# Two of the eight loads of a's rows per piece issued by GpSimd instead of SyncE

## The chip, the cores and the metric

The kernel runs on one core of a Trainium2 chip. The metric is the device time of one execution in microseconds (us), as the median of several executions. The engines of the core are TensorE (PE, its weight loads shown apart as PEld), VectorE (DVE), ScalarE (ACT), GpSimd (POOL) and SyncE (SP). DMA transfers are issued by SP or by POOL, each in the order of its own instruction stream, and run on the core's 16 DMA engines.

## What is computed

The reference, cut to what matters, for 8 batches, 8 heads, 576 positions, a head width of 64 and 32 memory slots:

```
a = exp(phi - max over positions);  a = a / (sum over positions + 1e-9)
k_m = einsum('bhsm,bhsd->bhmd', a, k)
v_m = einsum('bhsm,bhsd->bhmd', a, v)
attn = softmax over the 32 slots of (q @ k_m^T) / sqrt(64)
x = attn @ v_m, heads side by side: 8 x 576 x 512
score = x @ w_gate; of each batch the 128 rows with the highest score:
    x[row] += sigmoid(score) * (relu(x[row] @ w1) @ w2)
```

The change concerns `v_m`, the sum over the positions of a times v.

## The kernel before

Everything runs on one core, and the order of each engine's instructions is fixed when the program is built: generators (`batch`, `split_v`, `sums`, `attention_beside`, `load_weights`, `forward`) are stepped in turn by a loop at the end of the function, each with its own rate, and what they emit goes into the engines' streams in that order.

Per batch, `softmax` computes a on DVE and ACT. `keys` turns a round with PE (line 303), splits it into a coarse and a fine part (`aS` and `alo`), and stores both parts twice in the DRAM buffer `aparts` with eight DMAs from POOL (line 314). It also computes k_m with PE (line 322). `split_v` does the same for v: a load into `vb` on SP (line 271), the split on DVE, and stores to `vparts` from POOL (line 290).

`values` then computes v_m for a set of four batches at a time, so there are two stages of sums. A stage walks over the 576 positions in 24 pieces of T = 24 positions. Of a piece, `load` (lines 340 to 352) brings v's rows into the buffer `v_rows` with two DMAs of 384 KB from POOL (line 345), and a's rows into `a_rows` with eight DMAs of 48 KB from SP (line 350): four blocks `j`, two groups `g` each. There are two buffers of each kind (NB = 2). The piece is 96 small matmuls on PE (line 371), 24 for each of the four accumulators `acc`. `load` of piece c is written into the program after the first four matmuls of piece c-1, but it fills the buffer that piece c-2 has read, so SP and POOL wait for the last matmul of piece c-2 before they issue it. The pieces are numbered through here: 0 to 23 are the first stage, 24 to 47 the second.

Beside the loads of a's rows, SP issues all loads of inputs: `ph` (line 101), `kb` (105), `qb` (109), `vb` (271) and the weights. Beside the loads of v's rows, POOL issues the stores to `vparts` and `aparts`, the stores of the result (533) and the gathers and scatters of the chosen rows (594, 636). On each of the two queues there are eight semaphores for DMAs, used in turn: a DMA waits until the one issued eight places before it on its queue has landed.

In the first stage the sums alternate on PE with the keys of the batches 4 to 7; in the second with the attention of the batches 0 to 3 and the dense layers (lines 622, 629). After the second stage the attention of the batches 4 to 7 follows.

Of the kernel before, what the change touches and what calls it, by code (L numbers as in the profile page):

```python
# [44 lines left out]
def kernel(  # L45
# [14 lines left out]
    nc = tc.nc  # L60
# [273 lines left out]
    def values(st):  # L334

        accs = [accp.tile([P, 512], F32, name=f"acc{i}") for i in range(SET)]
        b0 = st * SET

        def load(ch):
            ss = slice(ch * T, (ch + 1) * T)
            vr, ar = v_rows[ch % NB].bitcast(F32), a_rows[ch % NB].bitcast(F32)
            for g in range(NG):
                nc.gpsimd.dma_start(  # L345
                    out=vr[g::2, :, g],
                    in_=vparts[g, b0:b0 + SET].rearrange("b t w j s d -> (b t w j) s d")[:, ss])
            for j in range(NPR):
                for g in range(NG):
                    nc.sync.dma_start(  # L350
                        out=ar[2 * j + g::8, j].rearrange("p s m -> p (s m)"),
                        in_=aparts[g, j, b0:b0 + SET].rearrange("b t w s m -> (b t w) (s m)")
                            [:, ch * T * M:(ch + 1) * T * M])


        n = S // T
        while len(keyed) < b0 + SET or min(split[b0:b0 + SET]) < NG * VC:
            yield
        for _ in range(4):
            yield  # L360
        for ch in range(NB - 1):
            load(ch)
            yield
        warm(warmth[st])
        yield
        for ch in range(n):
            vr, ar = v_rows[ch % NB], a_rows[ch % NB]
            for s in range(T):
                for bb in range(SET):
                    p = slice(bb * 32, bb * 32 + 32)  # L370
                    nc.tensor.matmul(out=accs[bb][:, :P].rearrange("p (j m) -> p j m", m=M),  # L371
                                     lhsT=vr[p, s].rearrange("p g d -> p (g d)"), rhs=ar[p, :, s],
                                     start=(ch == 0 and s == 0), stop=(ch == n - 1 and s == T - 1))
                if s == 0 and ch + NB - 1 < n:
                    load(ch + NB - 1)
                if s % 4 == 4 - 1:
                    yield
        for bb in range(SET):
            v_m[b0 + bb] = const.tile([P, P], F32, name=f"v_m{b0 + bb}")
            nc.scalar.activation(v_m[b0 + bb], accs[bb][:, :P], AF.Copy)  # L380
# [3 lines left out]
    def warm(n):  # L384

        if n:
            spare = bank([P, 512])
            for i in range(n):
                nc.tensor.matmul(out=spare, lhsT=ident16, rhs=wide[:, :512], start=True, stop=True)
# [406 lines left out]
```

## Time and profile before

| | us |
|---|---|
| median of 3 runs | 911.61 |
| the runs | 911.61, 912.07, 907.06 |
| the profiled execution | 907.15 |
| its span, first to last instruction | 905.3 |
| DVE busy in the span | 548.2 (61%) |
| PE busy in the span | 547.1 (60%) |
| POOL busy in the span | 258.7 (29%) |
| ACT busy in the span | 222.6 (25%) |
| mean rate of the DMAs | 183 GB/s |

The profiled execution is at the lower edge of the runs; 1.85 us of it lie outside the span. No engine is busy all the time. Up to 251 us DVE is busy nearly throughout with the softmaxes of the first batches; the two stages of sums run from 251 to 450 and from 475 to 721 us; the rest is attention and dense layers on PE and DVE. The profile puts a wait down to what ended it, and shows the chain of work that ended last, followed back from the end.

### The profile page before, as it was taken

The page shows a single profiled execution, that of the slowest core. Times are in us where ns is not written, and L with a number is a line of the kernel's source. Part 1 is how long each engine was busy: PE and PEld are TensorE (multiplying, and loading weights), DVE is VectorE, ACT ScalarE, POOL GpSimd, SP SyncE. Part 2 cuts the span into 40 slices and gives each one's busy share as a digit, 9 for nine tenths or more (in the row PEclk, how much of TensorE's full clock was granted, in tenths as well). Part 3 has the DMA queues.
Part 4 walks back from the last instruction along what each step waited for, and adds up shares of the span by engine and source line. Part 5 has one row for each costly group of instructions (what it writes and reads, how often), then busy time and mean ns, then how long its engine had stood idle before and what let it go on. Part 6 is the DMA issues. An engine that isn't in the chain of part 4 may idle for free.

```text
span 905.3 us, 16762 instructions
## 1 busy us (share of the span) xinstructions
PE 547.1 (60%) x6917; PEld 449.3 (50%) x6918; DVE 548.2 (61%) x803; ACT 222.6 (25%) x369; POOL 258.7 (29%) x373
## 2 busy tenths in 40 slices
PE   0010020202066568774859999987999798598595
PEld 0010020202065568774728787865885675476373
DVE  8997999999965386655914336206225347748800
ACT  2423242525213124222310120300210223134210
POOL 7245353425335224224142213223223011101100
PEclk9999999999999555557585555868569799589888
DMA  3569899896998677857777755546255433111200
GB/s 103 169 246 321 267 310 293 268 306 228 292 266 259 173 226 233 225 172 210 239 214 224 233 171 167 159 125 209 69 165 175 123 94 99 64 38 64 76 21 18
DMA packets 61409, 165.55 MB, mean 183 GB/s; under 512 B 12816, under 2 KB 21008, under 8 KB 61328
## 3 DMA queue, kind: packets, MB, share of 16 engines
q0 software_dynamic: 30080, 108.02, 37.2%
q1 hardware_dynamic: 31248, 56.39, 21.3%
q8 instruction: 57, 0.93, 0.4%
q14 instruction: 24, 0.20, 0.1%
HBM read 96.21 MB, written 68.16 MB: 182 GB/s over the span
## 4 chain that ended last, share of the span: by engine, by line
PE 45%; DVE 27%; DMA 15%; SPq 5%; issue 4%; POOL 1%; ACT 1%; DVEq 0%; POOLq 0%; ACTq 0%
PE acc L371 19%; PE bank L622 8%; DMA a_rows<-aparts 7%; PE bank L629 5%; SPq L350 5%; PE bank L522 4%; DMA aparts<-aS 3%; PE bank L505 3%; DVE mx L183 2%; DMA vparts<-vlo 2%; DVE vlo L287 2%; PE bank L585 2%; DVE ph L252 2%; DMA aparts<-alo 1%; PE bank L303 1%
## 5 line engine op out<-in xcount | busy, mean ns | idle before, releaser
L371 PE MATMUL acc<-a_rows,v_rows 32*128 32x128 f32 x4608 | 234.5, 374 | 114.1 <-DMA a_rows<-aparts 87.8
L371 PEld LDWEIGHTS acc<-a_rows,v_rows 32*128 32x128 f32 x4608 | 220.0, 285 | 142.6 <-issue 125.3
L345 POOL DMA_DIRECT2D v_rows<-vparts x96 | 92.4, 967 | 287.6 <-PE acc L371 278.6
L303 PE MATMUL bank<-ident,ph 128*96 128x128 f32 x96 | 23.3, 421 | 148.5 <-DVE ph L254 148.5
L303 PEld LDWEIGHTS bank<-ident,ph 128*96 128x96 f32 x96 | 17.5, 197 | 152.2 <-issue 145.6
L622 PE MATMUL bank<-xeT,w 128*128 128x128 f32 x512 | 78.4, 309 | 2.6 <-ACT xeT L612 2.1
L622 PEld LDWEIGHTS bank<-xeT,w 128*128 128x128 f32 x512 | 70.5, 216 | 8.3 <-ACT xeT L612 3.2
L290 POOL DMA_DIRECT2D vparts<-vlo x64 | 35.6, 559 | 123.6 <-DVE vlo L287 112.6
L566 DVE SCALAR_TENSOR_TENSOR marks<-row,tg,wide 128x576 bf16<-128x576 f32 x40 | 32.7, 818 | 58.6 <-ACT row L552 57.2
L526 DVE TENSOR_TENSOR xj<-bank,rd 128x512 f32<-128x512 f32 x40 | 27.3, 688 | 62.6 <-PE bank L522 62.4
L629 PE MATMUL bank<-w,hT 128*128 128x512 f32 x128 | 65.1, 647 | 0.0
L522 PE MATMUL bank<-vbd,eT 128*128 128x256 f32 x160 | 58.6, 505 | 0.3 <-ACT vbd L430 0.3
L206 DVE TENSOR_TENSOR num<-num,lin 128x1152 f32<-128x1152 f32 x16 | 21.7, 1358 | 37.8 <-ACT lin L170 36.5
L522 PEld LDWEIGHTS bank<-vbd,eT 128*128 128x128 f32 x160 | 36.7, 248 | 11.9 <-issue 5.0
L290 POOL DMA_DIRECT2D vparts<-vb x64 | 35.9, 565 | 9.6 <-DMA aparts<-aS 9.3
L629 PEld LDWEIGHTS bank<-w,hT 128*128 128x128 f32 x128 | 25.0, 206 | 24.2 <-issue 23.0
L533 POOL DMA_DIRECT2D out<-xj x24 | 16.2, 673 | 60.7 <-DVE xj L529 44.9
L634 DVE SCALAR_TENSOR_TENSOR ye<-bank,gr,xe 128x512 f32<-128x512 f32 x8 | 6.0, 748 | 43.7 <-PE bank L629 43.7
L430 ACT ACTIVATE vbd<-bank 32x128 f32<-32x128 f32 x32 | 8.6, 268 | 96.2 <-PE bank L426 95.9
L510 DVE TENSOR_SCALAR rd<-bank 128x40 f32<-128x40 f32 x8 | 1.6, 199 | 50.5 <-PE bank L505 50.5
L564 ACT ACTIVATE marks<-row,tg 128x576 bf16<-128x576 f32 x40 | 30.9, 773 | 1.3
L322 PE MATMUL bank<-kb,aS 96*32 96x64 f32 x768 | 19.3, 285 | 17.7 <-ACT aS L304 17.7
(128 smaller groups left out, 938.3 us busy)
## 6 DMA issues: line engine op xcount, KB each, us to landing
v_rows<-vparts POOLq DMA_DIRECT2D x96, 384.0 KB, 5.8
vparts<-vlo POOLq DMA_DIRECT2D x64, 288.0 KB, 4.3
vparts<-vb POOLq DMA_DIRECT2D x64, 288.0 KB, 5.2
a_rows<-aparts SPq DMA_DIRECT2D x384, 48.0 KB
vb<-in_v SPq DMA_DIRECT2D x32, 288.0 KB
kb<-in_k SPq DMA_DIRECT2D x16, 576.0 KB
aparts<-alo POOLq DMA_DIRECT2D x32, 288.0 KB, 7.9
aparts<-aS POOLq DMA_DIRECT2D x32, 288.0 KB, 8.5
```

The costliest lines, as they stand in the source:

```text
L290: nc.gpsimd.dma_start(out=view(vparts[g, b, t, w], c), in_=src)
L303: nc.tensor.transpose(out=tp[:, c], in_=a[:, c0 + c], identity=ident)
L345: nc.gpsimd.dma_start(out=vr[g::2, :, g], in_=vparts[g, b0:b0 + SET].rearrange("b t w j s d -> (b t w j) s d")[:, ss])
L350: nc.sync.dma_start(out=ar[2 * j + g::8, j].rearrange("p s m -> p (s m)"), in_=aparts[g, j, b0:b0 + SET].rearrange("b t w s m -> (b t w) ( ...
L371: nc.tensor.matmul(out=accs[bb][:, :P].rearrange("p (j m) -> p j m", m=M), lhsT=vr[p, s].rearrange("p g d -> p (g d)"), rhs=ar[p, :, s], s ...
L505: nc.tensor.matmul(out=den[:, c, g], lhsT=eT[:, g, c * P:(c + 1) * P], rhs=heads_of, start=True, stop=True)
L522: nc.tensor.matmul(out=o[:, g * 4 * Dh:(g + 1) * 4 * Dh], lhsT=eT[:, g, (c0 + c) * P:(c0 + c + 1) * P], rhs=vbd[b % 3][:, g].rearrange("p ...
L526: nc.vector.tensor_mul(x[:, c].rearrange("p (h d) -> p h d", d=Dh), o.rearrange("p (h d) -> p h d", d=Dh), rd[:, c0 + c].unsqueeze(2).to_b ...
L564: nc.scalar.activation(sign, row, AF.Sign, bias=g, scale=-1.0, accum_out=less[:, c:c + 1])
L566: nc.vector.scalar_tensor_tensor(out=cmp, in0=row, scalar=g, in1=wide[:, off:off + S], op0=ALU.is_equal, op1=ALU.mult, accum_out=equal[:, ...
L622: nc.tensor.matmul(out=ps[:, f, :n], lhsT=w1_sb[d][:, (f0 + f) * P:(f0 + f + 1) * P], rhs=xeT[:, d, :n], start=(d == 0), stop=(d == KD - 1))
L629: nc.tensor.matmul(out=ps[:n], lhsT=hT[:, f, :n], rhs=w2_sb[f // 2][:, f % 2], start=(f == 0), stop=(f == KF - 1))
```

## The change

```
             for j in range(NPR):
                 for g in range(NG):
-                    nc.sync.dma_start(
+                    eng = nc.gpsimd if 2 * j + g >= 8 - 2 else nc.sync
+                    eng.dma_start(
                         out=ar[2 * j + g::8, j].rearrange("p s m -> p (s m)"),
```

Of the eight loads of a's rows of a piece, the six with j = 0, 1, 2 stay on SP; the two with j = 3 are issued by POOL, behind the two loads of v's rows of the same piece. Sizes, addresses and buffers are the same. The lines below move by one, so line 350 becomes 351.

On SP, at the pieces 2 and 3 (the buffers `a_rows_99` and `a_rows_100` are the two of a's rows; a row with x8 is eight DMAs), before:

```order
L350 DMA a_rows_100<-aparts 16x768 x8
L105 DMA kb<-in_k 96x1536 x2
L271 DMA vb<-in_v 128x1x576
L350 DMA a_rows_99<-aparts 16x768 x8
L101 DMA ph<-in_phiT 128x576 x2
L350 DMA a_rows_100<-aparts 16x768 x8
```

and with the change:

```order
L351 DMA a_rows_100<-aparts 16x768 x6
L105 DMA kb<-in_k 96x1536 x2
L271 DMA vb<-in_v 128x1x576
L351 DMA a_rows_99<-aparts 16x768 x6
L101 DMA ph<-in_phiT 128x576 x2
L351 DMA a_rows_100<-aparts 16x768 x6
```

The order on SP is the same; each group of loads of a's rows is two shorter.

On POOL, at the pieces 5 to 7, where the eight stores of a batch's a stand between the loads (`v_rows_97` and `v_rows_98` are the two buffers of v's rows), before:

```order
L345 DMA v_rows_98<-vparts 64x24x64 x2
L314 DMA aparts<-alo 96x4x192 x2
L314 DMA aparts<-aS 96x4x192 x2
L314 DMA aparts<-alo 96x4x192 x2
L314 DMA aparts<-aS 96x4x192 x2
L345 DMA v_rows_97<-vparts 64x24x64 x2
L345 DMA v_rows_98<-vparts 64x24x64 x2
```

and with the change:

```order
L345 DMA v_rows_98<-vparts 64x24x64 x2
L351 DMA a_rows_100<-aparts 16x768 x2
L314 DMA aparts<-alo 96x4x192 x2
L314 DMA aparts<-aS 96x4x192 x2
L314 DMA aparts<-alo 96x4x192 x2
L314 DMA aparts<-aS 96x4x192 x2
L345 DMA v_rows_97<-vparts 64x24x64 x2
L351 DMA a_rows_99<-aparts 16x768 x2
L345 DMA v_rows_98<-vparts 64x24x64 x2
L351 DMA a_rows_100<-aparts 16x768 x2
```

Two loads of a's rows now stand ahead of the eight stores, and two behind each pair of loads of v's rows after them. The other engines' streams are unchanged.

## Rows read from the trace of the kernel before

**Rows 1.** The page's chain that ended last, by engine and by line.

```profile
PE 45%; DVE 27%; DMA 15%; SPq 5%; issue 4%; POOL 1%; ACT 1%; DVEq 0%; POOLq 0%; ACTq 0%
PE acc L371 19%; PE bank L622 8%; DMA a_rows<-aparts 7%; PE bank L629 5%; SPq L350 5%; PE bank L522 4%; DMA aparts<-aS 3%; PE bank L505 3%; DVE mx L183 2%; DMA vparts<-vlo 2%; DVE vlo L287 2%; PE bank L585 2%; DVE ph L252 2%; DMA aparts<-alo 1%; PE bank L303 1%
```

**Rows 2.** PE's longest waits, 251.3 to 450 us: total us, times, longest.

```profile
PE acc L371 <- DMA a_rows<-aparts: 61.2, 14, 24.8
PE acc L371 <- DMA aparts<-aS: 15.1, 2, 11.3
PE acc L371 <- DMA ph<-in_phiT: 10.3, 2, 5.3
```

**Rows 3.** PE's waits, 475 to 722 us, all of the sums.

```profile
PE acc L371 <- DMA a_rows<-aparts: 26.6, 6, 9.3
```

**Rows 4.** Busy time by stretch: PE, PEld, DVE, ACT, POOL, granted clock, DMA share, GB/s.

```profile
251.00:275.00 24.00, 16.16 (x288) 15.69 (x288) 12.36 (x14) 3.35 (x3) 7.46 (x11) 1.00 0.95 283
475.00:722.00 247.00, 229.15 (x2838) 186.92 (x2839) 91.12 (x186) 34.44 (x90) 57.46 (x65) 0.66 0.55 167
```

**Rows 5.** Lines 350 and 345: issue time in ns (min/median/max), first and last start.

```profile
L350 SPq DMA_DIRECT2D a_rows<-aparts x384: 471/587/2630, 240.0 to 706.5; - x192
L345 POOL DMA_DIRECT2D v_rows<-vparts x96: 953/955/1273, 237.9 to 702.3; - x96
```

**Rows 6.** Pieces 14 and 15, timeline of SP, POOL, PE: start us, us, what.

```profile
370.57 4.90 SPq L350 DMA_DIRECT2D a_rows<-aparts  x8
...
370.84 1.90 POOL L345 DMA_DIRECT2D v_rows<-vparts  x2 [7.54 <-PE acc L371]
...
368.55 1.97 PE L371 MATMUL acc<-a_rows,v_rows 32*128 32x128 f32 x32
371.44 5.39 PE L371 MATMUL acc<-a_rows,v_rows 32*128 32x128 f32 x96 [0.92 <-DMA a_rows<-aparts]
378.67 5.39 PE L371 MATMUL acc<-a_rows,v_rows 32*128 32x128 f32 x96 [1.84 <-DMA a_rows<-aparts]
```

**Rows 7.** Piece 12: v's two loads on POOL with their landings, and PE.

```profile
344.68 1.90 POOL L345 DMA_DIRECT2D v_rows<-vparts  x2 [4.74 <-PE acc L371]
...
DMA to landing us min/median/max: 4.4/4.9/5.5
...
352.07 1.97 PE L371 MATMUL acc<-a_rows,v_rows 32*128 32x128 f32 x32 [1.68 <-DMA a_rows<-aparts]
```

**Rows 8.** Pieces 1 to 3, timeline of SP and PE.

```profile
256.77 7.30 SPq L350 DMA_DIRECT2D a_rows<-aparts  x8
264.17 1.10 SPq L101 DMA_DIRECT2D ph<-in_phiT  x2
...
257.53 5.39 PE L371 MATMUL acc<-a_rows,v_rows 32*128 32x128 f32 x96 [0.80 <-DMA kb<-in_k]
267.93 5.39 PE L371 MATMUL acc<-a_rows,v_rows 32*128 32x128 f32 x96 [5.01 <-DMA ph<-in_phiT]
276.49 3.68 PE L371 MATMUL acc<-a_rows,v_rows 32*128 32x128 f32 x64 [3.17 <-DMA a_rows<-aparts]
```

**Rows 9.** Pieces 20 and 21, timeline of POOL and PE, landing of v_rows 416 to 419.

```profile
408.34 1.90 POOL L345 DMA_DIRECT2D v_rows<-vparts  x2 [7.53 <-PE acc L371]
...
416.95 1.93 POOL L345 DMA_DIRECT2D v_rows<-vparts  x2 [0.58 <-DMA aparts<-alo]
...
DMA to landing us min/median/max: 12.7/12.7/12.7
...
423.65 5.39 PE L371 MATMUL acc<-a_rows,v_rows 32*128 32x128 f32 x96 [11.33 <-DMA aparts<-aS]
...
431.40 5.39 PE L371 MATMUL acc<-a_rows,v_rows 32*128 32x128 f32 x96 [1.96 <-DMA a_rows<-aparts]
```

**Rows 10.** The page's group of the shortest DMAs on POOL, and a landing.

```profile
L290 POOL DMA_DIRECT2D vparts<-vlo x64 | 35.6, 559 | 123.6 <-DVE vlo L287 112.6
...
vparts<-vlo POOLq DMA_DIRECT2D x64, 288.0 KB, 4.3
```

## The prediction

> **What bounds the kernel now.** I read the chain that ended last first [rows 1]: it is led by PE, and the sums (line 371), the landing of a's rows and SP's issue of a's rows (line 350) are 19%, 7% and 5% of it. So the loads of a's rows stand on the path that sets the end with 12% of 905.3 us; v's rows, which come from POOL, are not among the leading entries. The reader is to see that DVE's 27% lies elsewhere, mostly ahead of the sums.
>
> The waits of PE say where. In the first stage of sums the three longest groups of waits for DMAs before line 371 come to 61.2 + 15.1 + 10.3 = 86.6 us [rows 2]; 24.8 of it is the wait before the very first piece, which leaves 61.8 us in the stage. In the second stage they are 26.6 us in 6 waits [rows 3], and PE is busy for 229.15 of 247 us there [rows 4]. Names such as aparts or ph in these waits are of what shared a semaphore or a queue; what PE needs there are a's and v's rows.
>
> How one load goes, in an undisturbed piece [rows 6]: piece 13 ends at 368.55 + 1.97 = 370.5 us, and frees the buffers for piece 15. SP issues its eight loads from 370.57 to 375.47, 0.61 us apart; POOL issues v's two from 370.84 to 372.74. PE starts piece 15 at 378.67, 8.1 us after the release, 3.2 us after SP's last issue, having waited 1.84 us. Which of the two came last? In piece 12 [rows 7] POOL issues at 344.68 and 345.63; the later landing takes 5.5 us, so v is there at 351.1 us, and PE starts at 352.07. The remaining 0.9 us are a's. So a is last, by SP's issue, and v stands only some 0.9 us behind it: that is about what is to be had per piece, before anything else binds.
>
> **What the change does, part by part.** SP: two issues fewer per piece. An issue takes 0.587 us in the median [rows 5], so SP's last one ends 2 × 0.6 = 1.2 us earlier: at release + 3.7 instead of + 4.9, and with the same 3.2 us to PE's start its six are there for a start at + 6.9.
>
> POOL: two issues more per piece, 96 in all. The trace of before has no load of this shape on POOL. Its cheapest DMAs take 0.559 us [rows 10], the two loads of v's rows 0.955 each [rows 5]; these have many short runs to write, the new ones 16 rows of 3 KB, so I take the near row, 0.56. The bounds are 0.56 and 0.955: POOL's fourth issue ends at release + 0.3 + 1.9 + 1.1 = + 3.3, or + 4.1 at the other end. When they land is the open price. POOL's transfers share a queue with v's two. Between the landings of v's two lie 0.95 + 5.5 - 4.4 = 2.05 us for 384 KB [rows 7]; at that rate 96 KB more take 0.5 us. So the four are there 0.5 us after v now, which is 0.9 - 0.5 = 0.4 us before a now. Bounds: if the two slip in beside v they cost nothing and the gain is 0.9; if each needs the 4.3 us from issue to landing that the shortest stores need, counted from a last issue start at + 2.8 to + 3.2, they land at + 7.1 to + 7.5, which is inside the same band; with the 5.5 of v's second load instead, + 8.3 to + 8.7, some 0.5 us later than a now. I take a gain of 0.5 us from release to start, and -0.5 and +0.9 as ends.
>
> This gain does not add up piece by piece. Where every piece waits, piece c starts a fixed time after the end of piece c-2, so 0.5 us less is had once in two pieces.
>
> First stage, cut at the three places at which a batch's eight stores to aparts stand between loads (pieces 5, 13 and 20):
> - Pieces 0 to 4. Here SP is late: at pieces 2 and 3 it also issues kb, vb and ph, and waits for semaphores; the eight loads of piece 2 take 7.30 us instead of 4.9, ph follows at 264.17, and piece 3's loads, whose buffer came free when piece 1 ended, at 257.53 + 5.39 = 262.9, go from 265.37 on. PE waits 5.01 and 3.17 us for these two [rows 8]. With six loads SP catches up 1.2 us at each of pieces 1, 2 and 3, and semaphores that stand eight places back are free earlier. Against that, the DMA engines are busy for 0.95 of this stretch [rows 4], so what SP gives may be taken by bandwidth. I take 4.5 us, about half of these 8.2 us and of the 1.2 us that piece 0's own issue gives; bounds 0 and 8.2.
> - Pieces 6 to 12. Seven pieces at 0.5 us every second one, 1.7 us, and once more a wait for kb and ph as above; I take 3.5.
> - Pieces 14 to 19: three times 0.5, of which I keep about half, 0.8, since not every piece waits (14 + 2 + 2 waits over the stage's 24 pieces [rows 2]).
> - Pieces 21 to 23, in the same way: 0.4.
> - Each of the three stretches of stores starts 2 × 0.56 = 1.1 us later, since POOL issues the two loads ahead of them: -3.3. The pieces around them show why gains stop here. Piece 20 waits 11.33 us, and piece 21 follows it; the loads of v's rows for piece 21 are issued at 416.95, behind the stores on the same queue, land 12.7 us later, and PE starts at 431.40 [rows 9]. With the change piece 20's loads of a's rows stand ahead of the stores and come many us earlier, but piece 21 still waits for v's rows, which move only as the stores move. So the 11 us are not gained; they move to piece 21.
>
> Sum of the first stage: 4.5 + 3.5 + 0.8 + 0.4 - 3.3 = 5.9 us.
>
> Second stage. Its first piece (24) waits 9.3 us [rows 3]: the loads wait for the last stores to aparts, then SP issues them; two issues fewer give 1.2 us. The other five waits come to 26.6 - 9.3 = 17.3 us. In these, PE waits for a as in piece 15, and 1.2 us of SP's issue come off each as long as v and POOL's two allow it: 5 × 1.0 = 5 us. On the other pieces PE has its own work (229.15 of 247 us), and the change does nothing. Sum 6.2 us. POOL's stores and gathers there are queued behind two more issues, at most 1.1 us each time; their readers (the dense layers) come several pieces later, so this I cost at nothing. If that cover were gone it would be 1.1 us on each of the four gathers of chosen rows (line 594) that POOL's stream has in this stage, 4.4 us.
>
> Together 12.1 us, and what follows the sums hangs on PE and moves with them. In the profiled execution that is 907.15 - 12.1 = 895.1 us. That execution is at the lower edge of the runs; against their median it is 911.61 - 12.1 = 899.5, which I round to 900.
>
> One rule speaks against this. The Trainium skill, DMA: Bandwidth & Descriptors, section "Issuing engines are not separate DMA queues", says that DMAs from any engine end on the same 16 DMA engines, and that issuing from several saves only the sequencer's time, usually small beside the transfer. Here the sequencer's time is not small: 8 × 0.587 = 4.7 of 8.1 us [rows 5, 6]; but the same DMA engines at 0.95 in one stretch [rows 4] agree with its first half. By it the sum would be the issue time alone where it is last, and nothing where transfers bind, which is the first rival.
>
> **The rivals.** *The transfers bind, not the issue.* The two loads go behind v on POOL's queue instead of beside it, and the bytes of a piece arrive when they arrive: a's last now at the start at + 8.1 less v's 0.9 ahead of it, plus 0.5 to 0.9 for 96 KB. Then the first stage gains 0 to 2 us less 3.3 at the stores, the second the 1 to 3 us of issue: within 3 us of now, 909 to 914. For it: DMA share 0.95 in pieces 1 to 3, and v only 0.9 us ahead of a. Against it: 0.55 in the second stage [rows 4].
>
> *POOL's two become the last ones.* Place: every piece, behind v's second load. Price: from issue to landing as long as v's second load, 5.5 us, gives a landing at + 8.3 to + 8.7, and a start some 0.5 us later than now, or more if the queue is filled by stores. It decides from a landing of the fourth at + 7.9 on. At 0.5 us on every second of the first stage's 24 pieces, 6 us, on the 6 that wait in the second, 3 us, and 3.3 us at the stores: 12.3 us, 911.6 + 12.3 = 924 us.
>
> *More is gained than I count.* If the stretches of stores don't hold the pieces (because a's rows, coming early, free SP and the DMA engines for the next piece), a third of the 11.33 us and of its two like is kept, 8 to 10 us more: some 890.
>
> That the change doesn't do what it says I hold for out: the streams show the two loads on POOL in every piece.
>
> **How the numbers follow.** A measurement of this kernel can tell about 0.5% from no change, that is 4.6 us: 907.0 to 916.2 is "same". Forecast 0.50, more gain 0.12, both faster: 0.62. Transfers bind 0.22: same. POOL's two last 0.16: slower. The likeliest case's own range is 893 to 907: its sum with pieces 0 to 4 at 0 to 8.2 and the second stage at 2 to 8. The range for 8 in 10 takes in half of the case of more gain, down to 888, and the case of no change, up to 915.
>
> **What would show it.** Right: PE's waits for a's rows fall from 61.8 to some 50 us in the first stage and from 26.6 to some 20 in the second; in a piece like 15, SP issues six loads in 3.7 us, and PE starts at release + 7.5 to 7.7; an issue of the new loads on POOL takes near 0.56 us; piece 20 hardly waits, and piece 21 waits longer. Wrong: PE's start moves to + 8.5 and its waits name the new loads of POOL; or the waits stay as long under other names; or piece 21 moves with piece 20, and the gain is larger.

## The result, and the profile after

The changed kernel takes 908.77 us in the median, beside 915.86 us for the kernel before on the same chips (20 runs each). Some runs of either kernel are slower as a whole; here and below a median is of all runs, and a ratio and the us gained or lost are of the others. The ratio is 0.988 with an interval of [0.985, 0.992]: 1.2% faster, or 10.7 us. The forecast was 12.1 us; its 900 us started from the first three runs of before, at 911.61, and from 915.86 the same 12.1 us lead to 903.8. The profiled execution of after took 903.99 us, with a span of 902.2 us.

In the page's chain that ended last, a's rows are still there: their landing has 11% of it where it had 7%, SP's issue 5% as before (line 371 of before is 372 now, and 350 is 351):

```profile
PE 46%; DVE 23%; DMA 17%; SPq 5%; issue 4%; POOL 2%; ACT 1%; DVEq 0%; POOLq 0%; ACTq 0%
PE acc L372 20%; DMA a_rows<-aparts 11%; PE bank L623 8%; PE bank L630 5%; SPq L351 5%; PE bank L523 4%; PE bank L506 3%; DMA aparts<-aS 2%; DMA vparts<-vlo 2%; PE bank L586 2%; DVE vlo L287 1%; DVE ph L252 1%; PE bank L460 1%; DVE xj L530 1%; DVE ph L191 1%
```

SP issues 288 loads of a's rows at 0.588 us each in the median, and POOL 96 at 0.520, by the view of the line (issue time in ns as min/median/max, first and last start):

```profile
L351 SPq DMA_DIRECT2D a_rows<-aparts x288: 471/588/2487, 237.2 to 692.2; - x144
L351 POOL DMA_DIRECT2D a_rows<-aparts x96: 502/520/546, 237.8 to 693.7; - x96
```

PE's waits in the two stages of sums (total us, times, longest), which answer [rows 2] and [rows 3]; two lines of the first stage, then the second stage's:

```profile
PE acc L372 <- DMA a_rows<-aparts: 75.7, 12, 24.3
PE acc L372 <- issue: 1.5, 2, 1.2
...
PE acc L372 <- DMA a_rows<-aparts: 25.4, 6, 11.9
```

The longest of the first stage, 24.3 us, lies ahead of the very first piece, as the 24.8 us did before. So 75.7 + 1.5 - 24.3 = 52.9 us are left in the stage, against 61.8 us. In the second stage the wait for the first piece (24) went up from 9.3 to 11.9 us, and the other five fell from 17.3 to 13.5 us.

The busy times of the two stages, from the first matmul of a stage's first piece to the end of its last (PE, PEld, DVE, ACT, POOL, granted clock, DMA share, GB/s), first of after, then of before:

```profile
247.70:441.90 194.20, 141.02 (x2632) 135.37 (x2633) 122.19 (x137) 53.21 (x61) 86.56 (x121) 0.92 0.78 227
469.10:716.00 246.90, 233.19 (x2830) 190.66 (x2830) 90.60 (x183) 33.63 (x86) 80.62 (x109) 0.65 0.54 166
```

```profile
251.30:449.80 198.50, 135.85 (x2632) 129.80 (x2632) 121.28 (x135) 52.64 (x60) 62.87 (x76) 0.63 0.75 220
475.40:721.00 245.60, 228.15 (x2830) 185.92 (x2830) 90.56 (x183) 33.50 (x85) 57.46 (x65) 0.66 0.55 168
```

A stretch less PE's busy time is its waiting: 62.6 to 53.2 us in the first stage and 17.4 to 13.7 in the second, together 13.2 us less. PE's busy time is 10.2 us more for nearly the same number of matmuls. This is why the two profiled executions lie only 3.2 us apart while the medians lie further. The further terms are small: the sums begin 3.6 us earlier, the gap between the stages is 1.6 us longer, and what follows them some 2 us longer. Whether the change has to do with the busy time comes up at the end.

The granted clock of the first stage differs too, 0.92 after and 0.63 before, but it isn't what shortens the stage: the 96 matmuls of a piece take 5.39 us at a granted clock of 0.50 (piece 15 of before [rows 6]) and at 1.00 (piece 17 of after), that is at 1.2 and at 2.4 GHz, and kernels below have first stages of 192.5 to 194.7 us at 0.60 and 0.61 (chosen pieces, input pieces). The rows are in the last section.

An undisturbed piece shows something the forecast did not say. Piece 18 of after: the timeline of SP, POOL and PE, then the landings from issue (min/median/max, us) of v's two, of POOL's two of a, and of SP's six:

```profile
384.63 3.64 SPq L351 DMA_DIRECT2D a_rows<-aparts  x6
384.91 1.95 POOL L345 DMA_DIRECT2D v_rows<-vparts  x2 [5.00 <-PE acc L372]
386.84 1.03 POOL L351 DMA_DIRECT2D a_rows<-aparts  x2
...
393.41 1.97 PE L372 MATMUL acc<-a_rows,v_rows 32*128 32x128 f32 x32 [3.21 <-DMA a_rows<-aparts]
...
DMA to landing us min/median/max: 4.7/5.6/6.5
DMA to landing us min/median/max: 5.7/5.7/5.7
DMA to landing us min/median/max: 2.0/4.0/5.6
```

SP is done 3.64 us after its first issue, as forecast. But PE starts 393.41 - 384.63 = 8.8 us after that issue, where piece 15 took 378.67 - 370.57 = 8.1 before [rows 6]. v's second load, issued at 385.9, lands 6.5 us later at 392.3. Of the others the view tells some landings only: POOL's first load, issued at 386.8, is there at 392.5, and the longest on SP, 5.6 us, is that of the fifth, issued at 387.1, there at 392.7. The semaphores of POOL's second and SP's sixth load are complete at 392.8 and 393.0. Everything arrives in the last microsecond or so, whoever issued it.

Around the input loads the picture is another. Pieces 2 to 6 on SP and PE, to be held against [rows 8]:

```profile
253.16 3.65 SPq L351 DMA_DIRECT2D a_rows<-aparts  x6
256.90 1.32 SPq L101 DMA_DIRECT2D ph<-in_phiT  x2
...
262.53 9.21 PE L372 MATMUL acc<-a_rows,v_rows 32*128 32x128 f32 x160 [4.29 <-DMA a_rows<-aparts]
...
299.63 1.97 PE L372 MATMUL acc<-a_rows,v_rows 32*128 32x128 f32 x32 [9.84 <-DMA a_rows<-aparts]
```

The loads of piece 2 take 3.65 us of SP where they took 7.30, ph follows at once, and PE no longer stops for 3.17 us ahead of piece 3. From the first matmul of the sums to the start of piece 6 it is 299.63 - 247.73 = 51.9 us; before it was 56.1.

Pieces 20 and 21 beside the stores, to be held against [rows 9]:

```profile
402.73 1.03 POOL L351 DMA_DIRECT2D a_rows<-aparts  x2
403.75 1.42 POOL L314 DMA_DIRECT2D aparts<-alo  x2
...
409.33 5.39 PE L372 MATMUL acc<-a_rows,v_rows 32*128 32x128 f32 x96 [4.56 <-DMA a_rows<-aparts]
...
410.75 1.93 POOL L345 DMA_DIRECT2D v_rows<-vparts  x2
...
421.57 4.75 PE L372 MATMUL acc<-a_rows,v_rows 32*128 32x128 f32 x84 [6.44 <-DMA a_rows<-aparts]
```

Piece 20's loads stand ahead of the stores now, and it waits 4.56 us instead of 11.33. Piece 21 waits for v's rows, which were issued behind the stores: 6.44 instead of 1.96. Of 13.3 us, 11.0 are left.

The second stage's waits, one by one, piece 24 first:

```profile
469.06 2.83 PE L372 MATMUL acc<-a_rows,v_rows 32*128 32x128 f32 x48 [11.88 <-DMA a_rows<-aparts]
517.12 3.68 PE L372 MATMUL acc<-a_rows,v_rows 32*128 32x128 f32 x64 [0.58 <-DMA a_rows<-aparts]
557.52 0.67 PE L372 MATMUL acc<-a_rows,v_rows 32*128 32x128 f32 x16 [0.86 <-DMA a_rows<-aparts]
579.62 0.94 PE L372 MATMUL acc<-a_rows,v_rows 32*128 32x128 f32 x16 [1.27 <-DMA a_rows<-aparts]
618.57 1.12 PE L372 MATMUL acc<-a_rows,v_rows 32*128 32x128 f32 x16 [4.16 <-DMA a_rows<-aparts]
695.49 2.83 PE L372 MATMUL acc<-a_rows,v_rows 32*128 32x128 f32 x48 [6.61 <-DMA a_rows<-aparts]
```

The kernel before waits 9.25, 1.45, 1.59, 2.50, 4.92 and 6.94 us, at the same places but for the second wait, which it has at piece 28 and not at 29. The five behind the first give 0.3 to 1.2 us each, 3.9 in all.

### The profile page after: what moved, and what is told of

Its sections match the earlier page's. It is cut to its first block, busy times and chain, and to the rows that moved or that the text cites. A ratio compares the mean times of both kernels' runs of the same rounds, so it can differ in the third digit from the quotient of the medians.

```text
span 902.2 us, 16769 instructions
## 1 busy us (share of the span) xinstructions
PE 557.9 (62%) x6917; PEld 461.4 (51%) x6918; DVE 544.4 (60%) x803; ACT 223.0 (25%) x369; POOL 311.2 (34%) x469
## 4 chain that ended last, share of the span: by engine, by line
PE 46%; DVE 23%; DMA 17%; SPq 5%; issue 4%; POOL 2%; ACT 1%; DVEq 0%; POOLq 0%; ACTq 0%
PE acc L372 20%; DMA a_rows<-aparts 11%; PE bank L623 8%; PE bank L630 5%; SPq L351 5%; PE bank L523 4%; PE bank L506 3%; DMA aparts<-aS 2%; DMA vparts<-vlo 2%; PE bank L586 2%; DVE vlo L287 1%; DVE ph L252 1%; PE bank L460 1%; DVE xj L530 1%; DVE ph L191 1%
## 5 line engine op out<-in xcount | busy, mean ns | idle before, releaser
L372 PE MATMUL acc<-a_rows,v_rows 32*128 32x128 f32 x4608 | 241.1, 383 | 103.0 <-DMA a_rows<-aparts 101.1
L372 PEld LDWEIGHTS acc<-a_rows,v_rows 32*128 32x128 f32 x4608 | 227.2, 294 | 131.1 <-issue 125.2
L623 PE MATMUL bank<-xeT,w 128*128 128x128 f32 x512 | 81.9, 319 | 2.6 <-ACT xeT L613 2.1
L623 PEld LDWEIGHTS bank<-xeT,w 128*128 128x128 f32 x512 | 73.8, 225 | 8.4 <-ACT xeT L613 3.2
L523 PE MATMUL bank<-vbd,eT 128*128 128x256 f32 x160 | 58.4, 504 | 0.3 <-ACT vbd L431 0.3
L351 POOL DMA_DIRECT2D a_rows<-aparts x96 | 49.5, 520 | 12.3 <-DMA aparts<-aS 11.4
```

Of the source, the lines that this page charges most:

```text
L351: eng.dma_start(out=ar[2 * j + g::8, j].rearrange("p s m -> p (s m)"), in_=aparts[g, j, b0:b0 + SET].rearrange("b t w s m -> (b t w) (s m) ...
L523: nc.tensor.matmul(out=o[:, g * 4 * Dh:(g + 1) * 4 * Dh], lhsT=eT[:, g, (c0 + c) * P:(c0 + c + 1) * P], rhs=vbd[b % 3][:, g].rearrange("p ...
L623: nc.tensor.matmul(out=ps[:, f, :n], lhsT=w1_sb[d][:, (f0 + f) * P:(f0 + f + 1) * P], rhs=xeT[:, d, :n], start=(d == 0), stop=(d == KD - 1))
```

## The experiments

Two theories stood against each other. By the theory of issue, SP's issue is last wherever PE waits, and the change gains in every such piece of both stages. By the theory of the crowded pieces, a piece that is alone is held by its transfers, and the gain lies in those few pieces of the first stage in which SP also issues inputs, or in which stores stand between. Of each diff against the kernel before only the lines that differ from the first one are shown; a median stands beside the kernel before's on the same chip, 917.6 to 917.7 us.

**One stage alone.**

```
-                    nc.sync.dma_start(
+                    eng = nc.gpsimd if st == 0 and 2 * j + g >= 8 - 2 else nc.sync
+                    eng.dma_start(
```

> The two loads go to POOL in the first stage of sums only (pieces 0 to 23); in the second stage SP issues all eight as before. Theory of the issue (as predicted: SP's shorter issue is worth 5.9 us in the first stage and 6.2 us in the second): about half of the change's gain, 5 to 6 us faster than before. Theory of the crowded pieces (a piece on its own gets its rows at the same time either way, and the gain comes only from pieces at which SP also issues inputs or the stores to aparts stand in the queues, nearly all of them in the first stage): nearly all of the gain, 8 to 11 us faster than before.

```
+                    eng = nc.gpsimd if st == 1 and 2 * j + g >= 8 - 2 else nc.sync
```

> The two loads go to POOL in the second stage only (pieces 24 to 47). Theory of the issue: 6 us faster than before. Theory of the crowded pieces: within 3 us of before, with PE's waits in the second stage at 23 to 28 us as now.

Measured: the first stage alone 906.93 us, ratio 0.990 [0.987, 0.994], 8.8 us less; the second alone 907.78 us, 0.991 [0.988, 0.995], 7.9 us less. Neither theory holds as it stood. The second stage is worth about as much as the first, which the theory of the crowded pieces denies. The two add up to 16.7 us and not to 10.7, but each is uncertain by some 3.5 us, and so is the change itself; that they don't add is not shown.

**How many loads.** Four on POOL instead of two:

```
+                    eng = nc.gpsimd if 2 * j + g >= 8 - 4 else nc.sync
```

> Four of a piece's eight loads on POOL instead of two. Theory of the issue: SP ends 1.2 us earlier still, but POOL's six are then the last ones, at release + 8.3 or later; slower than the change by 3 to 8 us. Theory of the crowded pieces: in a piece on its own the start stays at release + 8.0 to 8.8, and the pieces 2, 3, 9 and 10 gain a little more; within 4 us of the change, that is 7 to 14 us faster than before.

Measured: 919.48 us, 1.006 [1.002, 1.009], 5 us slower than before. Piece 8 shows why: the timeline of SP, POOL and PE, and between them the landings of POOL's four:

```profile
308.79 2.37 SPq L351 DMA_DIRECT2D a_rows<-aparts  x4
309.06 1.97 POOL L345 DMA_DIRECT2D v_rows<-vparts  x2 [5.96 <-PE acc L372]
311.02 1.98 POOL L351 DMA_DIRECT2D a_rows<-aparts  x4
...
DMA to landing us min/median/max: 8.4/8.7/9.1
...
322.90 8.41 PE L372 MATMUL acc<-a_rows,v_rows 32*128 32x128 f32 x152 [9.04 <-DMA a_rows<-aparts]
```

SP is done at 311.2, and the landings that the trace tells of POOL's four come 8.4 and 9.1 us after issue, at 319.4 and 321.1; PE starts 322.90 - 308.79 = 14.1 us after SP's first issue. The rival *POOL's two become the last ones* is true with four. But this piece has company: SP, free at 311.2, issues the two loads of kb (576 KB each), which land 8.9 and 11.7 us later. Where no inputs come in (pieces 10, 12 and 17 to 20) PE starts 7.9 to 9.3 us after the release, hardly later than with two. Which of the two, POOL's queue or the inputs that SP lets in earlier, costs the 5 us is not shown. Both forecasts missed, with 3 to 8 us slower than the change and within 4 us of it: it is some 16 us slower. Of none, two and four, two is the best.

**What is last in an undisturbed piece.** Two kernels take bytes away. The first leaves out the second of v's two loads (384 KB less per piece; the sums of its groups are then made of old values) and leaves all eight loads of a's rows on SP:

```
-            for g in range(NG):
+            for g in range(1):
```

> The kernel before without the second of v's two loads of a piece (g = 1), so 384 KB of 1152 KB are not moved; the eight loads of a's rows stay on SP. The computation lacks half of v. Looked at in an undisturbed piece such as 15. Theory of the issue: SP's last issue still ends at release + 4.9, and PE starts at release + 7.5 to 8.1 as before. Theory of the transfers: the rows of a arrive as the bytes allow; PE starts at release + 6.0 to 6.8, about the 1.3 to 2 us earlier that 384 KB take.

The second leaves out the two loads of a's fourth block (96 KB less; that block's products are made of old values), so SP issues six and POOL none in their place:

```
-            for j in range(NPR):
+            for j in range(NPR - 1):
```

> The kernel before without the two loads of a's fourth block: SP issues six, POOL v's two, and the 96 KB are not moved. The computation lacks the heads of the fourth block in v_m. In an undisturbed piece, theory of the issue: PE starts at release + 6.9 to 7.1. Theory of the transfers: SP's six land no sooner than v's second load, PE starts at release + 7.3 to 7.7. If the start is at + 8.0 or later, neither the issue nor the bytes of the two loads matter.

Measured in one run each: 898.53 and 896.50 us, beside 917.58. Piece 15 of the kernel with one load of v, and piece 23 of the kernel with six loads of a, SP and PE of each, and the loads in their pages (number, KB each, median us from issue to landing); first the former:

```profile
366.38 4.90 SPq L350 DMA_DIRECT2D a_rows<-aparts  x8
...
373.29 5.39 PE L371 MATMUL acc<-a_rows,v_rows 32*128 32x128 f32 x96 [1.84 <-DMA a_rows<-aparts]
...
a_rows<-aparts SPq DMA_DIRECT2D x384, 48.0 KB, 3.3
```

then the latter:

```profile
424.31 3.63 SPq L350 DMA_DIRECT2D a_rows<-aparts  x6
...
432.08 5.18 PE L371 MATMUL acc<-a_rows,v_rows 32*128 32x128 f32 x92 [2.69 <-DMA a_rows<-aparts]
...
a_rows<-aparts SPq DMA_DIRECT2D x288, 48.0 KB, 4.5
```

and the same entry of the changed kernel's page:

```profile
a_rows<-aparts SPq DMA_DIRECT2D x288, 48.0 KB, 4.9
```

With one load of v less, SP issues for as long as before, 4.90 us, and PE starts 6.9 us after the first issue; other undisturbed pieces of that kernel start at 6.5 (piece 7) and 6.7 (piece 23, without a wait). With two issues less, SP is done at 3.63, and PE starts at 7.8; pieces 7, 8, 12, 17 and 18 at 7.3 to 8.4, but 15, 16 and 20 at 9.4 to 9.7. So in these pieces SP's number of issues does not decide. That the bytes do is likely and not shown by itself: with a load of v one of POOL's issues, 0.955 us [rows 5], is gone too. The time from issue to landing points to the transfers: 3.3 us with half of v, 4.5 to 4.9 with all of it. The Trainium skill, DMA: Bandwidth & Descriptors, section "Issuing engines are not separate DMA queues", holds that DMAs from every engine share the same 16 DMA engines and that another issuer saves only the sequencer's time. For these pieces the trace agrees: SP's issue is 1.3 us shorter, and the starts at + 7.3 to 8.4 are next to before's + 7.6 to 8.5. The DMA share does not tell where that holds: from the release to PE's start it is 0.49 to 0.75 in such pieces of before's first stage (7, 12, 15, 18 and 22), and 0.56 to 0.78 in the four of its second stage that wait (28, 33, 36 and 39).

**Which pieces of the first stage.** The two loads on POOL only in pieces 0 to 3, 9, 10, 16 and 17, where SP has input loads at hand, then only in the pieces beside the stores:

```
+                    eng = nc.gpsimd if (st, ch) in NEAR and 2 * j + g >= 8 - 2 else nc.sync
+    NEAR = [(0, 0), (0, 1), (0, 2), (0, 3), (0, 9), (0, 10), (0, 16), (0, 17)]
```

> The two loads go to POOL only at eight pieces of the first stage, 0 to 3, 9, 10, 16 and 17, at and behind which SP also issues kb, ph or vb; on all others SP issues eight. Theory of the issue: 8 of 48 pieces, and the first cut of my sum: 4 to 5 us faster than before. Theory of the crowded pieces, if the inputs on SP are the crowd: 6 to 10 us faster than before; if it is the stores to aparts (pieces 5, 13, 20) that matter, 0 to 4 us.

```
+                    eng = nc.gpsimd if st == 0 and ch in NEAR and 2 * j + g >= 8 - 2 else nc.sync
+    NEAR = (4, 5, 12, 13, 19, 20)
```

> The two loads go to POOL only at the pieces 4, 5, 12, 13, 19 and 20 of the first stage, at and ahead of the three stretches of stores to aparts. If the stores are where the gain comes from, 4 to 7 us faster than before and PE's waits in the first stage at 55 to 57 us; if the inputs on SP are, as the run with eight pieces suggests, within 3 us of before and waits at 60 to 63 us.

Measured: 909.83 us, 0.993 [0.988, 0.997], and 915.03 us, 0.997 [0.992, 1.001]. Eight of 24 pieces bring 6.6 us of the first stage's 8.8. The pieces at the stores bring 3.1 us, which can't be told from nothing; the first stage of that trace waits 58.3 us, between the two forecasts, beside 62.6 before.

In the traces the first stage, with and without the two loads on POOL, cut at the starts of its pieces (us; the first column counts from the first matmul of the sums):

| kernel | to piece 6 | 6 to 14 | 14 to 21 | whole stage |
|---|---|---|---|---|
| before | 56.1 | 64.0 | 60.0 | 198.5 |
| second stage alone | 55.0 | 68.6 | 61.6 | 204.0 |
| after | 51.9 | 65.9 | 56.0 | 194.2 |
| first stage alone | 51.6 | 65.9 | 56.3 | 195.2 |
| input pieces | 50.3 | 65.2 | 59.6 | 194.7 |
| store pieces | 56.5 | 62.6 | 58.4 | 196.1 |
| chosen pieces (below) | 51.1 | 66.1 | 55.4 | 192.5 |

The first stretch gives 3 to 6 us in each kernel that has the loads on POOL from piece 0 on. The last gives 4 to 6 us in the two that have them in all pieces and in the chosen pieces, where of this stretch only piece 20 has them; 2 to 3 in the store pieces (19 and 20); and about nothing in the input pieces, which leave out piece 20. The middle one gives nothing against before; the 4.6 us between the two kernels that are alike there (the first two rows) show what such a stretch scatters by.

**Another engine.** The two loads on ACT, in both stages and then in the first stage only, with POOL in the second:

```
+                    eng = nc.scalar if 2 * j + g >= 8 - 2 else nc.sync
```

> The two loads are issued by ACT instead of POOL, so they go neither behind v's loads nor ahead of the stores to aparts, but ACT, which works through the softmaxes, waits for the release of the buffers with all that is queued behind. Theory of the issue, with POOL's queue as the price of the change: PE starts at release + 7.0 in undisturbed pieces. Theory of the transfers: at + 7.8 to 8.4 as now. On time: ACT's waits can cost more than this gives; 0 to 15 us slower than before, or if ACT has slack as fast as the change.

```
+                    eng = (nc.scalar, nc.gpsimd)[st] if 2 * j + g >= 8 - 2 else nc.sync
```

> The two loads are issued by ACT in the first stage and by POOL in the second. ACT's loads stand in no queue behind v's; in the run with ACT they landed at release + 4.5 to 5 and PE started at + 7.4 to 8.0 in undisturbed pieces of the first stage. Theory of the transfers: 11 to 16 us faster than before, level with the change or a little better. If ACT's waits hold back the softmaxes, 5 us or less faster than before.

Measured: 908.67 us, 0.986 [0.980, 0.991], and 909.00 us, 0.986 [0.978, 0.994]. Both lie level with the change. Piece 15 of the second kernel, where ACT issues the two, on SP, ACT and PE:

```profile
363.93 3.63 SPq L351 DMA_DIRECT2D a_rows<-aparts  x6
363.94 1.38 ACTq L351 DMA_DIRECT2D a_rows<-aparts  x2
...
371.92 5.39 PE L372 MATMUL acc<-a_rows,v_rows 32*128 32x128 f32 x96 [1.75 <-DMA a_rows<-aparts]
```

SP is done 3.63 us after its first issue and ACT earlier, and PE still starts at 371.92 - 363.93 = 8.0, as before's 8.1 with all eight on SP [rows 6]: the bytes are the same, the issue is 1.3 us shorter, and nothing is gained. The other undisturbed pieces of this stage (7, 8, 18 and 23) start at + 7.3 to 7.9, where the change has + 8.3 to 9.5. In such pieces POOL's queue may well cost some tenths of a us; in the time of the whole kernel these runs can't tell it.

**The disputed cost by itself.** Two more DMAs of 64 bytes per piece, with the eight loads left on SP: once issued by SP, once by POOL.

```
+    spare_col = const.tile([16, 96], F32, name="spare_col")
+            for i in range(2):
+                n = 2 * (st * (S // T) + ch) + i
+                nc.sync.dma_start(out=spare_col[:, n:n + 1], in_=w_gate[0:16].rearrange("(p o) -> p o", o=1))
```

> The kernel before with two more DMAs per piece on SP behind its eight, of 64 bytes each, so the issue is lengthened by 1.2 us and no bytes to speak of are added. Theory of the issue: the price of SP's issue with its sign turned, 9 to 12 us slower than before, and PE starts later in undisturbed pieces too if the eight were not done (they are, so any change there comes from the next piece's). Theory of the crowded pieces: nothing in undisturbed pieces, where SP waits for the release anyway; 3 to 6 us slower, from the pieces at which SP's loads come late.

The second has `nc.gpsimd` in the last line.

> The kernel before with two more DMAs per piece on POOL, behind everything of the piece, of 64 bytes each: the price on POOL's side alone. By my sum 3 x 1.1 us at the stores to aparts, 3 us slower than before. If the small DMAs' landings hold back POOL's later ones through the eight semaphores, 5 us or more slower; if POOL's place in the queue costs nothing, within 2 us of before.

Measured: on SP 948.18 us, 1.024 [1.013, 1.035] from two runs, 21.8 us slower, against 9 to 12 and 3 to 6 expected: both missed. On POOL 938.36 us, with runs from 920 to 944; there is no ratio, and the time stays open. PE's and SP's longest waits of the kernel with the two on SP:

```profile
PE acc L375 <- DMA a_rows<-aparts: 93.3, 13, 27.1
PE acc L375 <- DMA spare_col<-in_w_gate: 36.9, 13, 11.1
...
SPq L351 <- DMA a_rows<-aparts: 16.1, 23, 2.1
SPq L357 <- DMA a_rows<-aparts: 10.5, 11, 2.5
```

Before, SP waited 3.3 us in 7 waits for landings of a's rows, and here 26.6 us in 34. With ten DMAs to a piece and eight semaphores in turn, the ninth and the tenth have to wait for a load of the same piece. But that is not all of it: with the two on POOL, where SP issues eight as before, SP waits 18.9 us in 28 waits. In both kernels v's rows land later, 6.6 and 6.7 us after issue in the median of the pages, where before has 5.8; and PE starts late in undisturbed pieces, though SP's eight are issued by + 4.9 to 5.3: at + 9.1 to 9.8 (pieces 7, 11 and 15) with the two on SP, + 9.2 and 10.0 (12 and 11) with the two on POOL, instead of + 7.6 to 8.5. So the transfers are slower in both, by the small DMAs or by something else in these executions, and neither kernel prices SP's issue.

In the other kernel the page has POOL's two at 0.520 us of issue, as in the change:

```profile
L357 POOL DMA_DIRECT2D spare_col<-in_w_gate x96 | 49.5, 520 | 1.6 <-DMA v_rows<-vparts 0.9 <-DMA aparts<-aS 0.7
```

PE's waiting in its first stage is 62.9 us, as before's 62.6. So the 3.3 us that I charged for the two issues ahead of the stores are not seen in the waits; with the transfers slower as well, that does not say that they cost nothing.

**A choice of pieces.** From these runs a version: all of the second stage, and of the first only pieces 0 to 5, 9, 10, 13 and 20.

```
+                    eng = nc.gpsimd if (st == 1 or ch in NEAR) and 2 * j + g >= 8 - 2 else nc.sync
+    NEAR = (0, 1, 2, 3, 4, 5, 9, 10, 13, 20)
```

> The two loads go to POOL in the whole second stage, and in the first only at pieces 0 to 5, 9, 10, 13 and 20, where SP also issues inputs or POOL's stores to aparts follow; on the undisturbed pieces of the first stage SP issues eight. Theory of the issue: every piece left out gives up some 0.25 us, 14 pieces, so 3 to 4 us slower than the change. Theory of the crowded pieces: the undisturbed pieces lose some 0.5 us by the change (the traces show PE's start at release + 8.3 to 8.9 instead of + 7.6 to 8.3), so 2 to 4 us faster than the change, 12 to 15 us faster than before.

Measured: 909.86 us, 0.984 [0.979, 0.989], 14.7 us less. It is the largest gain of all, and its interval takes in the change's 0.988, so that it is better than the change is not shown. Leaving the two loads on SP in 14 undisturbed pieces did no harm.

## Why the prediction was right

The sign and the size were right, 10.7 us for 12.1. The mechanism was right in part, and that the sum came so near is in part luck: two misses hide in it. By its own terms the range of the likeliest case is 894 to 908 and not 893 to 907.

- **What bounds.** Right: PE waits for a's rows, and less so now. Of 61.8 us in the first stage 52.9 are left, for the 50 forecast. Of 26.6 in the second 25.4 are left, for 20.
- **Undisturbed pieces.** Wrong. "With the same 3.2 us to PE's start its six are there" was the step that failed. SP is done at + 3.6 as forecast, but PE starts at + 8.3 to 8.9 (pieces 8, 11, 16, 18, 20; piece 23 at + 9.5) instead of + 7.5 to 7.7; before it was + 7.6 to 8.5. It is no earlier; that the change makes it later isn't shown, since other traces with all eight on SP in these pieces have + 7.7 to 9.2. SP's issue doesn't bind there: with the two on ACT it is done at + 3.6 too, and the 3.2 us to PE's start become 4.4 in piece 15. The first rival was right for these pieces, as the two kernels with fewer bytes also show in the main.
- **POOL's two.** Right in the issue, 0.520 us for 0.56. Wrong in the landing: I held v's second load at its old place and put the two 0.5 us behind it, 0.4 us ahead of a's. But v's second load lands at + 7.3 to 8.0 in these pieces, where it landed at + 6.6 to 7.4 before, and the two come with the last of a, at + 7.8 to 8.6. The second rival had them at + 8.3 to 8.7. With four on POOL they are last.
- **Pieces 0 to 4.** Right: 4.5 less 1.1 forecast, 4.2 found.
- **Pieces 6 to 12.** 3.5 less 1.1 forecast, nothing found against before (64.0 to 65.9 us), in a stretch that scatters by more than the term.
- **Pieces 14 to 20 and the stores.** The wait moved from piece 20 to piece 21, as forecast, and 2.3 of 13.3 us were kept. But the stretch gave 4 us where I counted 0.8 less 1.1: I charged the two issues ahead of the stores in full and kept nothing of the early loads, and one of these or both were too dark. This made up for pieces 6 to 12; that is the luck.
- **Second stage.** The five waits gave 3.9 us for 5 in this pair of traces. Over eight traces it is 3: the waits behind piece 24's are 17.4, 21.6, 17.3 and 16.7 us with eight loads on SP (before, first stage alone, input pieces, store pieces), and 13.7, 15.9, 14.4 and 16.8 with two on POOL (after, second stage alone, chosen pieces, and ACT with POOL). I took the five to be alike, and they aren't. At piece 33, where SP's eight take 5.8 to 7.1 us, the wait goes from 1.6 to 3.2 us down to 0.9 to 1.5, and piece 28 is like it. At pieces 36 and 39, where the eight go out in 4.9, it is 0 to 2.5 and 4.6 to 5.1 us against 1.3 to 2.9 and 4.1 to 5.0, little or nothing. The 1.2 us of piece 24 weren't there: its wait was 8.1 to 12.1 us in all the traces, 9.3 before, 11.9 after, and 11.8 with six loads and none on POOL. It doesn't follow the issue.

What stays open is where the second stage alone gets its 7.9 us, with an interval of 4.2 to 11.5. The 3 us of waiting lie below it.

## What to carry to other kernels

When an issuing queue seems last, see what the load takes from issue to landing when it is issued earlier: here, where the queue had nothing else to do, loads issued 1.3 us sooner landed no sooner, though the DMA engines were busy for only half to three quarters of that time. What a second issuer gave lay at the few places where the first has other loads in its stream, where stores stand between, or where its loads take longer to go out than they do undisturbed. Moving two of eight helped, moving four cost 5 us. Look at more than one pair of traces, and at several pieces of each: a piece's start scatters by more than the term that was forecast. Read the gain of such a change from the waits, stage by stage, and its size from the medians, since one pair of profiles can differ by more in PE's busy time than the change is worth.

## What the runs showed of the hardware

**PE's busy time in the second stage.** The same 2830 matmuls took 221 to 242 us in eleven profiles, and they took longer the lower the granted clock of the stage was, from 0.69 down to 0.62 (share of 2.4 GHz, between the levels). The second stage of the kernel with four loads on POOL, and of that with one load of v, in the columns of [rows 4]:

```profile
475.40:718.70 243.30, 221.41 (x2830) 179.49 (x2830) 90.59 (x183) 33.49 (x85) 103.47 (x157) 0.69 0.56 172
```

```profile
471.10:712.20 241.10, 231.28 (x2830) 189.55 (x2830) 90.17 (x183) 33.51 (x85) 35.62 (x43) 0.65 0.44 135
```

| second stage, us | length | PE busy | waiting | clock |
|---|---|---|---|---|
| four loads on POOL | 243.3 | 221.4 | 21.9 | 0.69 |
| first stage alone | 244.7 | 223.1 | 21.6 | 0.68 |
| before | 245.6 | 228.2 | 17.4 | 0.66 |
| input pieces | 245.2 | 227.9 | 17.3 | 0.66 |
| ACT in the first, POOL in the second | 251.0 | 234.2 | 16.8 | 0.64 |
| store pieces | 258.5 | 241.8 | 16.7 | 0.62 |
| second stage alone | 241.8 | 225.9 | 15.9 | 0.66 |
| chosen pieces | 244.8 | 230.4 | 14.4 | 0.65 |
| after | 246.9 | 233.2 | 13.7 | 0.65 |
| six loads of a | 245.2 | 233.8 | 11.4 | 0.64 |
| one load of v | 241.1 | 231.3 | 9.8 | 0.65 |

Nine of these rows look as if what PE doesn't wait were taken back by a lower clock: the length stays within 241 to 247 us while the waiting goes from 21.9 to 9.8. The other two don't fit: four kernels that wait 16.7 to 17.4 us have PE busy for 227.9 to 241.8. So the busy time goes with the clock, and that the clock goes with the waiting is not shown. The forecast took every us of waiting in this stage as won; a difference of this size in the busy time can hide it in any one pair of profiles.

**Clock and pieces.** The 96 matmuls of a piece, when they run through, take 5.39 us at 1.2 and at 2.4 GHz alike. The stretch of the first stage with piece 15 of before [rows 6], and the same stretch of after with its piece 17:

```profile
370.00:390.00 20.00, 13.28 (x241) 12.80 (x240) 19.23 (x25) 4.99 (x6) 6.02 (x6) 0.50 0.84 230
```

```profile
370.00:390.00 20.00, 16.65 (x308) 16.33 (x304) 13.47 (x20) 4.92 (x5) 9.16 (x12) 1.00 0.66 183
...
384.81 5.39 PE L372 MATMUL acc<-a_rows,v_rows 32*128 32x128 f32 x96 [0.22 <-issue]
```

**Two small DMAs more per piece.** Two DMAs of 64 bytes per piece on SP cost 2.4%, with SP's waits for landings at 26.6 us instead of 3.3. With the two on POOL these waits are 18.9 us, and in both kernels v's rows land some 0.9 us later; what slows the transfers is not shown.
